# Tap products by two channels side by side in place of four, with a smaller home and a new instruction order

## The chip, the cores and the metric

The kernel runs on one core of one Trainium2 chip. The metric is the device time of one execution in microseconds. The names of the engines are those of the profile: PE is TensorE (its weight loads have a row of their own, PEld), DVE is VectorE, ACT is ScalarE, POOL is GpSimd, SP is SyncE, which here only issues DMAs.

## The reference

One block of a sequence model on 2048 positions of 512 channels in bf16: a state-space convolution and an MLP, each behind a layer norm (the MLP has a second one of its own), each added to its input.

```python
def _A_ref(u, A_re, A_im, B_re, B_im, C_re, C_im, log_dt, Dskip):
    dt = jnp.exp(log_dt)[:, None]
    A = A_re + 1j * A_im;  Bc = B_re + 1j * B_im;  Cc = C_re + 1j * C_im
    logdA = dt * A;  dB = dt * Bc
    l = jnp.arange(L)                                    # L = 2048, rounded to bf16
    P = jnp.exp(logdA[:, :, None] * l[None, None, :])    # 512 x 128 x 2048
    K = jnp.einsum("dn,dnl,dn->dl", Cc, P, dB).real      # the taps, one row per channel
    # y = causal convolution of u with K along the sequence, by FFT of length 4096
    return y + u * Dskip[None, None, :]

def _B_ref(x, w1, b1, w2, b2):                           # 512 -> 1376 -> 512
    y = _layernorm(x, axis=-1)
    h = _gelu(jnp.einsum("bsd,df->bsf", y, w1) + b1)
    return jnp.einsum("bsf,fd->bsd", h, w2) + b2

x = A_u
h = x + _A_ref(_layernorm(x), ...)
h2 = h + _B_ref(_layernorm(h), ...)
```

## The kernel before, in words

All data lives in one SBUF tile `ar` (the "arena"), in which every named buffer is a byte range, and in four PSUM tiles of 128 x 1024 f32 (`ps`), which are handed out as slots. So nearly every row of the profile reads `ar<-ps`, `ps<-ar` or `ar<-ar`, and lines tell the steps apart.

The stages, in the order of their work:

- *Parameters* (L635 to L1070). The raw parameters are loaded and transposed, and `bexps` (L801), `aexps` (L1000 to L1007) and `chain` (L1050 to L1073) make two tables of complex powers: A with 20 rows (a coarse position) and B with 33 rows (a step of 8), each for 128 states (the partitions) and 512 channels in four chunks `c` of 128. Their cosines and sines come from ScalarE (L1068) in `hf` 0 (chunks 0 and 1) and `hf` 1 (chunks 2 and 3), and VectorE multiplies them in (L1030, and L1072 for the A table of chunks 2 and 3). That table lies in `EA2` and `IA2` with the order chunk, group of channels `g` (4), row (20, padded with zeros to 32), channel `i` (32); channel `32 g + i` of the A table belongs to channel `4 i + g` of the columns of the B table.
- *Taps*. K at position `256 h + 8 k + r` is the sum over the states of A times B, which is a matmul for one channel: 20 rows of A as weights, 33 columns of B moving, once for the real and once for the imaginary parts. `kgen` (L1101, L1102) does this for chunks 0 and 1 with four channels in four column groups of the array. `kgen4` (L1132, L1133) does it for chunks 2 and 3 with four channels in one matmul: 4 x 32 = 128 weight columns, 33 x 4 = 132 moving columns, of whose 128 x 132 results only the four blocks on the diagonal (own rows, own channel) are used. All of them are evicted (`evac`, on ScalarE as L542 or on VectorE as L544) into the home `Kg[1]`, and L1142 adds the skip term `Dz`.
- *Spectra of the taps*. `carry` (L1152) shifts rows of the home by four small DMAs, `kspec` (L1167) and `fstage` (L981) transform it, with a trip through DRAM between them (`AK_d`, written and read by `kstage`); `lstage` (L1195, L1214) makes the part for the second half of the sequence. `q` 0 is chunks 0 and 1, `q` 1 is chunks 2 and 3.
- *Convolution*. `unorm` (L947, L949) and `xspec` (L961) norm and transform the input of a half `b` of the sequence, `inverse` multiplies by the taps' spectrum (L1243 to L1251, VectorE) and transforms back (L1259), and a transposing DMA (L1265, `turn`) brings each chunk back to positions.
- *Tail and MLP*. `tail` (L1324 to L1365) finishes the transform, adds the residual and takes the second pair of norms; `mlp` (L1383, L1385 the GELU, L1405, L1407 and the output DMAs) runs for four quarters of 512 positions.

In `stats`, which both norms use, the inverse square root is a power on GpSimd (L926), on which VectorE then waits (L619, L928 in the code).

The order in which each engine gets its instructions is written out. Each step registers an operation with `add`, which numbers it, takes its engine or its two possible engines and a planned cost, and works out its dependencies from the byte ranges. `ORDER` lists the numbers in the order of issue; a negative number `~i` is operation `i` on its second engine. A planner (`Sched.run`) goes through the list with the planned costs; it only decides which PSUM slot a result gets and where TensorE, when it would stand idle in the plan, gets filler matmuls that compute nothing (L1510, at most 24 in a gap). Each engine runs its own list strictly in that order.

Of the kernel before, what the change touches and what calls it, by code (L numbers as in the profile page):

```python
# [15 lines left out]
P = 128  # L16
# [149 lines left out]
class VS(V):  # L166
# [244 lines left out]
def kernel(ctx, tc, A_u, A_A_re, A_A_im, A_B_re, A_B_im, A_C_re, A_C_im, A_log_dt, A_Dskip,  # L411
# [88 lines left out]
    Kg = [take(bf16, NB, 2, 32), at(sc0 - 512, bf16, NB, 4, 2, 32)]  # L500
# [418 lines left out]
    def stats(stv, buf, n, eps1, eps0, pr):  # L919

        sa = lambda k: (lambda: stv.ap()[:, :, k])
        TT(buf[0], stv, stv, ALU.subtract, n=n, aap=sa(1), bap=sa(4), pr=pr)
        STT(buf[2], stv, 512.0 * eps0 / eps1, stv, ALU.add, ALU.add, n=n, aap=sa(2), bap=sa(5), pr=pr)
        STT(buf[1], buf[0], 0.25 * eps1, buf[0], ALU.mult, ALU.mult, n=n, pr=pr)
        STT(buf[1], buf[2], eps1 / 512.0, buf[1], ALU.mult, ALU.add, n=n, pr=pr)
        POOL(0.3, lambda: gp.tensor_tensor(buf[3].ap(), buf[1].ap(), mhalf.ap().to_broadcast([P, n]), ALU.pow), r=[buf[1], mhalf], w=[buf[3]], pr=pr)  # L926
        TT(buf[5], stv, stv, ALU.add, n=n, aap=sa(1), bap=sa(4), pr=pr)
        STT(buf[4], buf[5], -0.5, buf[3], ALU.mult, ALU.mult, n=n, pr=pr)  # L928
# [188 lines left out]
    def kgen4(c, pr):  # L1117
        Ar, Br, Ai, Bi = EA2[c - 2], EB[c], IA2[c - 2], IB[c]
        kg = Kg[1]
        for j0 in range(0, 32, 6):  # L1120
            S.pr = pr + 0.01 * (j0 // 6)
            p = Ps()
            n = min(6, 32 - j0)
            h = (n + 1) // 2
            for b in range(2):
                def fn(e, p=p, j0=j0, b=b, h=h):
                    for jj in range(h):
                        i = j0 + h * b + jj
                        o = pst(p)[:, 512 * b + 132 * jj:512 * b + 132 * jj + 132].rearrange("p (k g) -> p k g", g=4)
                        w = lambda v: v.ap().rearrange("p g a i -> p (g a) i")[:, :, i]  # L1130
                        x = lambda v: v.ap()[:, :, 4 * i:4 * i + 4]
                        pe.matmul(o, lhsT=w(Ar), rhs=x(Br), start=True, stop=False)  # L1132
                        pe.matmul(o, lhsT=w(Ai), rhs=x(Bi), start=False, stop=True)  # L1133
                add("PE", 0.13 * h, fn, r=[EA2, Br, IA2, Bi], w=[p], new=[p] if b == 0 else [], hv=1)
# [4 lines left out]
            def ifn(p=p, h=h):  # L1139
                return pst(p).rearrange("p (b q) -> p b q", b=2)[:, :, 0:132 * h].rearrange("p b (i n) -> p n b i", i=h)  # L1140
            evac(ofn, ifn, 2 * h * 4 * NB, [p], [kg])
        add("DVE", c_dve(128), lambda e: dve.tensor_tensor(kg.ap()[:, 0, :, c & 1, :], kg.ap()[:, 0, :, c & 1, :], Dz.ap()[:, c, :].unsqueeze(1).to_broadcast([P, 4, 32]), ALU.add), r=[kg, Dz], w=[kg])  # L1142

    def kgof(q, g):
        return Kg[0].ap() if q == 0 else Kg[1].ap()[:, :, g]
# [406 lines left out]
```

## Time and profile before

| | us |
|---|---|
| median of 3 runs (lowest, highest) | 235.97 (235.88, 236.08) |
| the profiled execution | 235.89 |
| its span | 234.0 |
| PE busy in it | 200.7 (86%), 2809 matmuls |
| PEld busy | 106.9 (46%) |
| ACT busy | 177.3 (76%), 217 instructions |
| DVE busy | 170.0 (73%), 304 instructions |
| POOL busy | 39.8 (17%) |
| mean granted clock of TensorE | 0.997 |

A line of the groups reads: line, engine, operation, what it writes and reads with shapes, count, busy time in us and mean of one in ns, idle time ahead of it and what ended that. A line of the timeline gives start and length in us. A line of the chain does so too, of the work that ended last. A row of the stretches gives the stretch and its length, then the busy time and the count of each engine, the granted clock, the share of the 16 DMA engines and GB/s.

### The profile page before, as it was taken

The numbers are of one execution on the slowest core, as the hardware profiler recorded it, in microseconds if no ns is written. First come the engines' busy times: TensorE is split into PE (matmuls) and PEld (weight loads), VectorE is DVE, ScalarE is ACT, GpSimd is POOL, SyncE is SP. The second block draws the span as 40 slices with busy tenths as digits, with TensorE's granted clock in tenths as the row PEclk, the third lists the DMA queues.
The fourth block names the chain that finished last, engine by engine and source line by source line (L and its number), as shares of the span: only waits on it lengthen the run. The fifth ranks groups of instructions, "written<-read, shape, count | busy, mean of one in ns | idle before, by whom it ended". The sixth has DMA issues, their size and how long they took to land.

```text
span 234.0 us, 6711 instructions
## 1 busy us (share of the span) xinstructions
PE 200.7 (86%) x2809; PEld 106.9 (46%) x2809; DVE 170.0 (73%) x304; ACT 177.3 (76%) x217; POOL 39.8 (17%) x185
## 2 busy tenths in 40 slices
PE   4206898868888899999989988899999999999993
PEld 2102633325666685456753343344444444444552
DVE  4969989998997764798999889889934884022021
ACT  5999999999999898999989897787275106806600
POOL 7950760000055520040000110100000101000000
PEclk9999999999999999999999999999999999999998
DMA  5692220100000163875589922235632072053103
GB/s 170 165 197 55 59 36 11 37 1 3 3 6 6 30 146 68 244 202 183 112 140 198 311 96 41 49 66 104 114 66 38 0 139 66 0 111 79 34 20 72
DMA packets 39246, 20.33 MB, mean 87 GB/s; under 512 B 26738, under 2 KB 37012, under 8 KB 39216
## 3 DMA queue, kind: packets, MB, share of 16 engines
q1 hardware_dynamic: 38510, 19.28, 36.1%
q0 software_dynamic: 256, 0.30, 0.8%
q8 instruction: 22, 0.36, 0.6%
q10 hardware_dynamic: 450, 0.33, 0.5%
q14 instruction: 8, 0.07, 0.1%
HBM read 8.10 MB, written 4.49 MB: 54 GB/s over the span
## 4 chain that ended last, share of the span: by engine, by line
PE 41%; ACT 13%; DVE 7%; DMA 5%; issue 4%; POOL 3%; SPq 1%; ACTq 0%; DVEq 0%
PE ps L1405 16%; PE ps L1383 13%; ACT ar L542 9%; DMA ar<-ar 3%; PE ps L1329 2%; ACT ar L1068 2%; DMA ar<-AK_d 2%; PE ps L1259 2%; PE ps L981 2%; ACT ar L1385 2%; DVE ar L1248 2%; DVE ar L1243 1%; POOL ar L926 1%; PE ps L961 1%; POOL ar L1466 1%
## 5 line engine op out<-in xcount | busy, mean ns | idle before, releaser
L542 ACT CAST ar<-ps 128x1024 bf16<-128x1024 f32 (+3 forms) x75 | 66.6, 965 | 11.8 <-PE ps L1259 5.1
L1385 ACT ACTIVATE ar<-ps,ar 128x512 bf16<-128x512 f32 (+1 forms) x44 | 28.6, 687 | 25.0 <-PE ps L1383 24.5
L1383 PE MATMUL ps<-ar 128*128 128x512 bf16 (+1 forms) x176 | 40.4, 379 | 1.5 <-ACT ar L542 1.1
L1405 PE MATMUL ps<-ar 128*128 128x512 bf16 (+3 forms) x187 | 39.6, 367 | 0.0
L1068 ACT ACTIVATE ar<-ps 128x1024 bf16<-128x1024 int16 x36 | 34.5, 1058 | 0.5 <-PE ps L1059 0.5
L1407 DVE TENSOR_TENSOR ar<-ps,ar 128x512 bf16<-128x512 f32 (+1 forms) x17 | 10.8, 653 | 29.5 <-PE ps L1405 16.3
L1243 DVE TENSOR_TENSOR ar<-ar 128x2048 bf16<-128x2048 bf16 x24 | 28.8, 1220 | 3.8 <-PE ps L1259 3.0
L1405 PEld LDWEIGHTS <-ar 128*128 128x128 bf16 (+1 forms) x187 | 18.0, 98 | 19.9 <-issue 0.4
L1383 PEld LDWEIGHTS <-ar 128*128 128x128 bf16 (+1 forms) x176 | 17.1, 100 | 21.7 <-issue 3.0
L1059 PE MATMUL ps<-ar 128*32 128x512 f16 (+1 forms) x368 | 21.6, 331 | 5.7 <-ACT ar L1068 5.6
L544 DVE CAST ar<-ps 128x1024 bf16<-128x1024 f32 (+3 forms) x20 | 21.2, 1075 | 7.0 <-PE ps L1133 3.0
L1510 PE MATMUL ps<-ar 128*128 128x512 bf16 x53 | 14.6, 412 | 13.6 <-DMA ar<-in_A_u_dram 12.2
L1030 DVE TENSOR_TENSOR ar<-ar 128x2048 bf16<-128x2048 bf16 x21 | 24.8, 1214 | 0.8 <-ACT ar L1068 0.4
L926 POOL TENSOR_TENSOR ar<-ar 128x4 f32<-128x4 f32 (+1 forms) x6 | 9.3, 1544 | 93.9 <-DVE ar L603 42.2
L801 ACT ACTIVATE ar<-ar 128x1024 bf16<-128x1024 f32 x16 | 15.7, 1041 | 1.1 <-DVE ar L613 1.1
L1059 PEld LDWEIGHTS <-ar 128*32 128x32 f16 x368 | 9.3, 97 | 15.8 <-issue 13.5
L961 PE MATMUL ps<-ar 128*32 128x512 bf16 x256 | 15.9, 380 | 0.2 <-ACT ar L542 0.2
L1259 PE MATMUL ps<-ar 64*128 64x128 bf16 x384 | 13.6, 217 | 1.1 <-ACT ar L542 1.1
L1510 PEld LDWEIGHTS <-ar 128*128 128x128 bf16 x53 | 4.9, 102 | 21.0 <-issue 17.5
L1259 PEld LDWEIGHTS <-ar 64*128 64x128 bf16 x384 | 11.1, 94 | 6.7 <-issue 2.7
L619 DVE SCALAR_TENSOR_TENSOR ar<-ar 128x4 f32<-128x4 f32 (+5 forms) x37 | 10.2, 282 | 5.3 <-POOL ar L926 3.5
L981 PE MATMUL ps<-ar 128*32 128x512 bf16 (+1 forms) x256 | 13.0, 328 | 0.2
(118 smaller groups left out, 293.7 us busy)
## 6 DMA issues: line engine op xcount, KB each, us to landing
ar<-in_A_u_dram SPq DMA_DIRECT2D x4, 512.0 KB
AK_d<-ar SPq DMA_DIRECT2D x4, 512.0 KB
ar<-AK_d SPq DMA_DIRECT2D x4, 512.0 KB
out_dram<-ar SPq DMA_DIRECT2D x30, 64.0 KB
ar<-in_B_w_dram SPq DMA_DIRECT2D x4, 344.0 KB
ar<-ar SPq DMA_DIRECT2D x20, 64.0 KB
ar<-in_B_w_dram SPq DMA_DIRECT2D x2, 640.0 KB
AL_d<-ar POOLq DMA_DIRECT2D x8, 36.0 KB, 4.0
```

What stands on the lines that cost most here:

```text
L542: act.copy(out_fn(), in_fn())
L544: dve.tensor_copy(out_fn(), in_fn())
L961: pe.matmul(pst(p)[32 * cg:32 * cg + 32, 512 * z:512 * z + 512], lhsT=BD.ap()[:, 32 * f + 2 - 2 * jl:32 * f + 34 - 2 * jl], rhs=un[2 * (2 ...
L1030: dve.tensor_tensor(o, o[:, 1].unsqueeze(1).to_broadcast([P] + list(o.shape[1:])), f[:, :, ::-1, ::-1] if rev else f, ALU.mult)
L1059: pe.matmul(pst(p)[32 * g:32 * g + 32, 256 * j:256 * (j + n)].rearrange("p (a b) -> p a b", a=n), lhsT=W2[DELTAS.index(d)].ap(), rhs=S2[g] ...
L1068: add("ACT", c_act(1024), lambda e, o_=o_, i_=i_: act.activation(o_(), i_(), ACT.Sin, scale=SINSC), r=[p, TBL], w=[sc[cs]])
L1243: dve.tensor_tensor(pieces(o).rearrange("p z (a r d) -> p a z r d", a=4, r=2), k, x, ALU.mult)
L1259: pe.matmul(pst(p)[:, 512 * h + 128 * k:512 * h + 128 * k + 128], lhsT=o[z].ap()[rows, k, r, :], rhs=TP[w].ap()[rows, f0 // 2 + k, :], sta ...
L1383: pe.matmul(pst(p)[:fs, 512 * z:512 * z + 512], lhsT=w1s[dc].ap()[:, fc * P:fc * P + fs], rhs=ybuf.ap().rearrange("p (t c) k -> p c t k", ...
L1385: add("ACT", c_act(512, 1), lambda e, p=p, z=z, fc=fc, fs=fs: act.activation(hT.ap()[:fs, fc, :], pst(p)[:fs, 512 * z:512 * z + 512], ACT. ...
L1405: pe.matmul(pst(p)[:, 512 * z + c0:512 * z + c1], lhsT=hT.ap()[:fs, fc, 128 * t:128 * t + 128], rhs=w2s[fc].ap()[:fs, c0:c1], start=(fc == ...
L1510: pe.matmul(slots[z][:, 0:512], lhsT=identb.ap(), rhs=hs[15].ap(), start=True, stop=True)
```

## The change

- `kgen4` is replaced by `kgen2`: each matmul of four channels (128 weight columns by 132 moving columns) becomes two matmuls of two channels (64 by 66), one in the left and one in the right half of the array's columns (`tile_position=(0, 32 * g)`, g = 0 and 2). Real and imaginary parts are accumulated as before. Per chunk these are 128 matmuls in place of 64.
- Half as many results come out, so a PSUM tile holds 12 channels `i` of each group in place of 6: per chunk three evictions (792, 792 and 528 columns) in place of six (five of 792 and one of 264).
- The home `Kg[1]` has 33 x 2 x 2 x 32 entries per partition in place of 33 x 4 x 2 x 32; channel group `g` is read from column `g & 1` (`kgof`). It begins 512 bytes later.
- The planned costs change: kgen2's are 0.14 us per `i` (kgen4's 0.13), and the power in `stats` is planned with 1.5 us in place of 0.3.
- `ORDER` is another list, of 946 in place of 964 operations. Operations 402 to 439 (kgen4) become 402 to 421 (kgen2), and those above 439 have numbers lower by 18. Among the differences: the third DMA that ACT issues, operation 4, stands ahead of the table load (11) in place of behind it; 78 (the eviction of L820, 1024 columns) goes from DVE to ACT and 115 (a copy of 512 columns, L611) from ACT to DVE; the power (162) stands ahead of the memset of L1466 (286) in place of behind it; the read of chunks 0 and 1 from DRAM (374) stands ahead of the carries of chunks 2 and 3 (422 to 425) in place of behind them; the first inverse on PE (521 before, 503 after) stands ahead of the xspec matmuls of the second half in place of behind five of them; the loads of `B_w2` stand ahead of those of `B_w1`.

```diff
-    Kg = [take(bf16, NB, 2, 32), at(sc0 - 512, bf16, NB, 4, 2, 32)]
+    Kg = [take(bf16, NB, 2, 32), at(sc0, bf16, NB, 2, 2, 32)]
...
-        POOL(0.3, lambda: gp.tensor_tensor(buf[3].ap(), buf[1].ap(), mhalf.ap().to_broadcast([P, n]), ALU.pow), r=[buf[1], mhalf], w=[buf[3]], pr=pr)
+        POOL(1.5, lambda: gp.tensor_tensor(buf[3].ap(), buf[1].ap(), mhalf.ap().to_broadcast([P, n]), ALU.pow), r=[buf[1], mhalf], w=[buf[3]], pr=pr)
...
-        for j0 in range(0, 32, 6):
+        for j0 in range(0, 32, 12):
...
-            n = min(6, 32 - j0)
-            h = (n + 1) // 2
+            h = min(12, 32 - j0) // 2
...
-                        o = pst(p)[:, 512 * b + 132 * jj:512 * b + 132 * jj + 132].rearrange("p (k g) -> p k g", g=4)
-                        w = lambda v: v.ap().rearrange("p g a i -> p (g a) i")[:, :, i]
-                        x = lambda v: v.ap()[:, :, 4 * i:4 * i + 4]
-                        pe.matmul(o, lhsT=w(Ar), rhs=x(Br), start=True, stop=False)
-                        pe.matmul(o, lhsT=w(Ai), rhs=x(Bi), start=False, stop=True)
-                add("PE", 0.13 * h, fn, r=[EA2, Br, IA2, Bi], w=[p], new=[p] if b == 0 else [], hv=1)
+                        for g in range(0, 4, 2):
+                            o = pst(p)[32 * g:32 * g + 64, 512 * b + 66 * jj:512 * b + 66 * jj + 66].rearrange("p (k g) -> p k g", g=2)
+                            w = lambda v: v.ap()[:, g:g + 2].rearrange("p g a i -> p (g a) i")[:, :, i]
+                            x = lambda v: v.ap()[:, :, 4 * i + g:4 * i + g + 2]
+                            pe.matmul(o, lhsT=w(Ar), rhs=x(Br), start=True, stop=False, tile_position=(0, 32 * g))
+                            pe.matmul(o, lhsT=w(Ai), rhs=x(Bi), start=False, stop=True, tile_position=(0, 32 * g))
+                add("PE", 0.14 * h, fn, r=[EA2, Br, IA2, Bi], w=[p], new=[p] if b == 0 else [])
...
-            evac(ofn, ifn, 2 * h * 4 * NB, [p], [kg])
+            evac(ofn, ifn, 2 * h * 2 * NB, [p], [kg])
...
-        return Kg[0].ap() if q == 0 else Kg[1].ap()[:, :, g]
+        return Kg[0].ap() if q == 0 else Kg[1].ap()[:, :, g & 1]
```

More of the change, by code (lines that the diff above doesn't have):

```diff
@@ L1115, in kgen, with kgen2 @@
         add("DVE", c_dve(32), lambda e: dve.tensor_tensor(kg.ap()[:, 0, c & 1], kg.ap()[:, 0, c & 1], Dz.ap()[:, c, :], ALU.add), r=[kg, Dz], w=[kg])
-    def kgen4(c, pr):
+    def kgen2(c, pr):
         Ar, Br, Ai, Bi = EA2[c - 2], EB[c], IA2[c - 2], IB[c]
         kg = Kg[1]
-        for j0 in range(0, 32, 6):
-            S.pr = pr + 0.01 * (j0 // 6)
+        for j0 in range(0, 32, 12):
+            S.pr = pr + 0.01 * (j0 // 12)
             p = Ps()
-            n = min(6, 32 - j0)
-            h = (n + 1) // 2
+            h = min(12, 32 - j0) // 2
             for b in range(2):
@@ L1139, in ifn @@
             def ifn(p=p, h=h):
-                return pst(p).rearrange("p (b q) -> p b q", b=2)[:, :, 0:132 * h].rearrange("p b (i n) -> p n b i", i=h)
-            evac(ofn, ifn, 2 * h * 4 * NB, [p], [kg])
-        add("DVE", c_dve(128), lambda e: dve.tensor_tensor(kg.ap()[:, 0, :, c & 1, :], kg.ap()[:, 0, :, c & 1, :], Dz.ap()[:, c, :].unsqueeze(1).to_broadcast([P, 4, 32]), ALU.add), r=[kg, Dz], w=[kg])
+                return pst(p).rearrange("p (b q) -> p b q", b=2)[:, :, 0:66 * h].rearrange("p b (i n) -> p n b i", i=h)
+            evac(ofn, ifn, 2 * h * 2 * NB, [p], [kg])
+        add("DVE", c_dve(64), lambda e: dve.tensor_tensor(kg.ap()[:, 0, :, c & 1, :], kg.ap()[:, 0, :, c & 1, :], Dz.ap()[:, c, :].unsqueeze(1).to_broadcast([P, 2, 32]), ALU.add), r=[kg, Dz], w=[kg])
     def kgof(q, g):
-        return Kg[0].ap() if q == 0 else Kg[1].ap()[:, :, g]
+        return Kg[0].ap() if q == 0 else Kg[1].ap()[:, :, g & 1]
     def carry(q, pr):
@@ L1472 @@
         for c in (2 * q, 2 * q + 1):
-            (kgen if q == 0 else kgen4)(c, 5.1 + 4 * c)
+            (kgen if q == 0 else kgen2)(c, 5.1 + 4 * c)
         carry(q, 9.1 + 8 * q)
```

66 rows, old and new, of the table ORDER are left out of this document.

## The prediction

> **What bounds the kernel now.** I read the page's head first, then the busy time by stretches, then the chain that ended last, then the rows of the stage that the change touches.
>
> ```profile
> span 234.0 us, 6711 instructions
> PE 200.7 (86%) x2809; PEld 106.9 (46%) x2809; DVE 170.0 (73%) x304; ACT 177.3 (76%) x217; POOL 39.8 (17%) x185
> ...
> 77.00:89.70 12.70, 12.70 (x212) 10.23 (x216) 8.12 (x20) 11.64 (x15) 4.23 (x5) 1.00 0.44 105
> 89.70:117.60 27.90, 27.70 (x648) 16.21 (x640) 23.33 (x26) 25.64 (x29) 2.40 (x4) 1.00 0.63 163
> 117.60:154.00 36.40, 32.38 (x397) 15.04 (x390) 32.11 (x50) 32.51 (x41) 2.61 (x3) 1.00 0.54 131
> ...
> 124.00:136.00 12.00, 3.25 (x14) 1.20 (x15) 1.00 0.96 272
> 136.00:154.00 18.00, 2.19 (x10) 0.69 (x8) 1.00 0.17 34
> ```
>
> In the three rows of stretches the columns after the length are PE, PEld, DVE, ACT, POOL. The last two rows are the filler matmuls of L1510 alone (PE, then PEld). From 77.0 to 117.6 TensorE is never free (40.4 of 40.6 us), while VectorE has 4.6 and 4.6 us to spare and ScalarE 1.1 and 2.3. From 117.6 to 154 TensorE lacks 4.0 us, and 24 of its matmuls there are fillers that compute nothing: its slack is before the MLP, not where the taps are made.
>
> ```profile
> 79.05 0.23 PE ps L1132
> ...
> 85.88 3.76 ACT ar L542 x5
> ...
> 93.38 4.98 DMA ar<-AK_d
> ...
> 111.36 6.11 DMA ar<-ar
> ...
> 126.83 0.97 PE ps L1510 x4
> 127.80 0.55 PE ps L1329 x4
> ```
>
> The chain goes from the products of kgen4 (L1132, L1133) through ScalarE's evictions of them, the Dz addition, the four carries, the trip of the spectra through DRAM, the first transpose (L1265) and the evictions held up by it, to the first tail (L1329), ahead of which four fillers ran. Whatever brings that tail and then the MLP forward is worth its time at the end.
>
> **The change part by part.** The sum is made against the profiled execution (235.89 us, span 234.0 us, so 1.89 us around it); the median of the runs is 235.97, 0.08 above.
>
> *Evictions and home.*
>
> ```profile
> L1132 PE MATMUL ps<-ar 128*128 128x132 bf16 x64 | 8.7, 229 | 0.0
> L1133 PE MATMUL ps<-ar 128*128 128x132 bf16 x64 | 8.6, 227 | 0.0
> L1101 PE MATMUL ps<-ar 128*20 128x33 bf16 x256 | 9.8, 247 | 0.0
> L542 ACT CAST ar<-ps 128x792 bf16<-128x792 f32 x7 | 5.5, 871 | 0.2 <-PE ps L1133 0.2
> L544 DVE CAST ar<-ps 128x792 bf16<-128x792 f32 x3 | 2.8, 974 | 1.3 <-PE ps L1133 1.3
> L544 DVE CAST ar<-ps 128x264 bf16<-128x264 f32 x2 | 1.0, 498 | 1.7 <-PE ps L1133 1.7
> L1059 PEld LDWEIGHTS <-ar 128*32 128x32 f16 x368 | 9.3, 97 | 15.8 <-issue 13.5
> L1329 PEld LDWEIGHTS <-ar 128*64 128x64 bf16 x48 | 2.4, 109 | 3.5 <-issue 2.2
> L1383 PEld LDWEIGHTS <-ar 128*96 128x96 bf16 x16 | 1.9, 122 | 1.5
> ```
>
> Twelve evictions (5.5 + 2.8 + 1.0 = 9.3 us) become six: by the new order one of 792 columns on VectorE (0.97), three of 792 (2.6) and two of 528 on ScalarE. The 528s lie between the 264 and 792 rows (0.5 and 0.87); I take 0.6, since 528 is two thirds of 792. Sum 4.8, so 4.5 us less on two engines, 1.7 on ScalarE and 2.8 on VectorE. On the path this is worth little: TensorE has no gap for it to close before 117.6, and VectorE idles there. Bounds: 0, and 2.2 (half of 4.5, were both engines the limit). The halved Dz addition and the smaller home cost nothing: the Dz addition stays one instruction per chunk on an engine with time to spare, and the readers of the home read as many rows as before.
>
> *The products on TensorE.*
>
> ```profile
> 84.00:88.00 4.00, 4.00 (x32) 3.98 (x32) 1.00 0.44 109
> ...
> 70.06 0.29 PE L1101 MATMUL ps<-ar 128*20 128x33 bf16 x4
> ...
> 70.61 0.28 PE L1101 MATMUL ps<-ar 128*20 128x33 bf16 x4
> ```
>
> The first row counts L1132 alone: 32 in 4.00 us, so a pair (four channels) takes 0.125 us and kgen4's 64 pairs 8.0 us. The change makes 256 matmuls of 64 x 66 out of 128 of 128 x 132: per four channels two pairs, one in each half of the array. No row has this shape. The nearest is kgen: its four column groups run side by side (x4 in a row), and from 70.06 to 70.61 (four such rows on) four channels of each group take 0.55 us, so a round of four matmuls takes 0.069 (L1101 and L1102 have one each). 33 columns are a quarter of 132, and yet kgen4's single matmul takes 0.0625: a round costs nearly the same at both sizes. Two rounds per four channels give 0.1375 us, 64 x 0.1375 = 8.8: **+0.8 us**, with no cover, since TensorE is full. Bounds: if each matmul costs only its share of kgen's round (0.069 / 4 = 0.017), 4 x 0.017 x 64 = 4.4 us, -3.6; if the cost follows the weight columns, 0.017 x 64 / 20 = 0.055 each, 14.1 us, +6.1. I stay by the round, since the shapes on either side of the new one both have it.
>
> The Trainium skill, "TensorE: Matmul & The Clock Gate", section "LDWEIGHTS", puts a weight load at columns / 1.2 ns, and "TensorEngine Tiling (Array Packing)", section "Restrictions and Gotchas", says that column tiling excludes Fast Weight Load. By these kgen4's fast load is given up for four slow ones of 53 ns, an estimate of 64 x 4 x 53 ns = 13.7 us if they follow one another. The trace agrees only in part: the loads of 32, 64 and 96 columns last 97, 109 and 122 ns, 0.4 ns per column, half of what that rule says; what they cost one behind the other at this size no row shows. That case is the first rival below.
>
> *The order of the front.*
>
> ```profile
> 1.70 1.28 ACT L536 ACT_TABLE_LOAD   x1 [1.70 <-PEq L1536]
> 1.73 0.41 ACTq L554 DMA_DIRECT2D ar<-in_A_B_re_dram  x1
> ...
> 19.84 0.61 ACT L611 ACTIVATE ar<-ar 128x512 f16<-128x512 f32 x1
> ...
> 7.30 1.22 DVE L544 COPY ar<-ps 128x1024 bf16<-128x1024 bf16 x1
> ...
> 74.47 2.00 ACT L1068 ACTIVATE ar<-ps 128x1024 bf16<-128x1024 int16 x2
> ...
> 73.32 0.17 DVE L619 SCALAR_TENSOR_TENSOR ar<-ar 128x8 f32<-128x8 f32 x1 [1.48 <-POOL ar L926]
> 77.61 1.16 DVE L1072 TENSOR_TENSOR ar<-ar 128x2048 bf16<-128x2048 bf16 x1
> ```
>
> ScalarE carries the path up to its last sine (ends 76.5). In the new order its third DMA issue (0.41) stands ahead of the table load, +0.4; the 1024-column copy of L820 moves from VectorE to it (about +1.0 in its row of casts) and a 512 copy (0.61) leaves: +0.4. So its last sine ends near 77.3. The last product of the taps' inputs (L1072) began only at 77.6, 1.1 us after that sine, since VectorE had lost 1.48 us to GpSimd's power (L926), which was queued behind the memset of L1466; the new order puts it ahead of that memset and eight VectorE instructions before its reader. VectorE then follows ScalarE at once: 77.3 in place of 77.6, **-0.3**. Bounds: -1.1 (ScalarE does not slip) and +0.8 (VectorE, which takes over several GpSimd instructions, is as late as before).
>
> *The order of the middle.*
>
> ```profile
> 89.91 3.35 SPq L1152 DMA_DIRECT2D ar<-ar  x4
> ...
> 89.00:90.00 1.00, 1.00 (x28) 0.50 (x20) 0.34 (x2) 0.90 (x2) 0.00 (x0) 1.00 0.01 2
> ...
> 140.28 1.02 PE L1383 MATMUL ps<-ar 128*128 128x512 bf16 x4 [0.51 <-ACT ar L542]
> ...
> ar<-in_B_w_dram SPq DMA_DIRECT2D x4, 344.0 KB
> ...
> ar<-in_B_w_dram SPq DMA_DIRECT2D x2, 640.0 KB
> ...
> 88.63 2.77 PE L961 MATMUL ps<-ar 128*32 128x512 bf16 x48
> ...
> 118.63 1.07 PE L1259 MATMUL ps<-ar 64*128 64x128 bf16 x32 [0.89 <-ACT ar L542]
> 120.46 1.07 PE L1259 MATMUL ps<-ar 64*128 64x128 bf16 x32 [0.22 <-ACT ar L542]
> ```
>
> On SP's queue the first read of chunks 0 and 1 from DRAM (374) moves ahead of the four carries of chunks 2 and 3 (3.35 us); what it waits for, the write of those chunks, has landed by 89 (the DMA share is 0.01 from 89 to 90), and the carries can't start before 89.9, so nothing behind it waits. Behind the transposes the two 640 KB loads of the MLP's second weights now stand ahead of the four of 344 KB that its first matmul needs: 2.66 MB at the 272 GB/s of the row from 124 to 136 are 9.8 us, from about 122.5 to 132.3, still ahead of an MLP that begins at 140.3 now and near 138.5 then (L1383): 0, with 6 us to spare. On TensorE the first inverse (chunk 0) moves ahead of five eight-matmul blocks of L961 (0.46 each, 2.77 / 6), so its transposes can start some 2 us earlier than 111.36, and the eviction that waited for the 6.11 us transpose is no longer late: the gaps of 0.89 and 0.22 close, **-1.1**. The four fillers ahead of the tail (0.97) go, because their wait was the same row of transposes: **-1.0**. Bounds: 0 for both, and -2.9 more (4.0 us of idle time in the third stretch less the 1.1). After the tail the new order has the same instructions in nearly the same places; I count 0. The new planner cost of the power (1.5 for 0.3) moves only fillers and slots.
>
> Sum: -0.3 + 0.8 - 1.1 - 1.0 = -1.6; 235.9 - 1.6 = **234.3 us**.
>
> **The rivals.**
> 1. *Weight loads set the pace* (the other side). The upper bound of the products, +6.1 in place of +0.8: 234.3 + 5.3 = 239.6. For it: a load of 64 columns is longer than one of 32 (109 against 97 ns), and at this size there is little streaming (66 columns) to hide it. Against: kgen's groups run side by side. It decides from 0.1625 us per four channels (0.1375 + 1.6 / 64); from there on the change is slower. The rule of the Trainium skill's page "TensorE: Matmul & The Clock Gate", section "LDWEIGHTS", speaks for this rival.
> 2. *Nothing closes.* TensorE is full from 77 to 117.6, and the gaps behind have another cause (DMA share 0.96 from 124 to 136). Then -0.3 + 0.8 remains: 236.4, at the edge of no change.
> 3. *Issue sets the pace.* -3.6 in place of +0.8, 4.4 us more; ScalarE has only 3.3 us to spare up to 117.6 and the trip through DRAM keeps its length, so I let half of it through: 232.1.
>
> **How the numbers follow.** Forecast 0.46, rival 3 0.12, rival 2 0.17, rival 1 0.13; 0.12 for the bounds of the front and of the middle that add up to a loss. So faster by over 0.2% (0.47 us, about what a measurement of this kernel can tell) 0.58, within it 0.17, slower 0.25. The forecast alone spans 232.8 to 235.4. The range reaches from rival 3 with a little of the bound of the middle, 231.8, to rival 2 with the front 1.1 later (+0.8 in place of -0.3), 237.5, and 0.3 of slower products, 237.8; rival 1's full price is left out.
>
> **What would show it.** The 256 products of kgen2 should fill 8 to 9.5 us of TensorE, less the blocks of other work among them, against 13 or more in rival 1 and under 5 in rival 3; six evictions of 4.8 us; no wait of VectorE for L926 near 70 us; the last sine near 77.3; the first transpose issued near 109; the first tail near 126 with no fillers ahead; from there to the end as long as before. The prediction is wrong if the products take over 10.5 us, if the gaps ahead of L1259 and the fillers stay, or if the MLP begins as late as now.

## The result and the profile after

The changed kernel takes **251.39 us** (median of 4 runs, 251.21 to 251.71) against 235.94 us (235.88 to 236.08) for the kernel before on the same chip: a ratio of **1.0656**, 95% interval 1.0637 to 1.0674, or 15.45 us more. The prediction said 234.3 us, with 237.8 as its upper end, and named the side wrong. The profiled execution took 251.21 us (span 249.4).

The head of the page after, with the 40 slices of TensorE and of its granted clock (tenths; a slice is 6.2 us):

```profile
span 249.4 us, 6968 instructions
PE 213.6 (86%) x2940; PEld 115.9 (46%) x2940; DVE 175.9 (71%) x308; ACT 172.9 (69%) x209; POOL 35.1 (14%) x183
PE   3225898969888999999999995798999999999993
PEclk9999599999999855799999999799999999999999
```

Before, the clock row was 9 nearly throughout. Now it falls in three places: slice 5 (the front), slices 14 to 17 (the tap products) and slice 26 (the start of the MLP).

Busy time by stretches of the changed kernel (PE, PEld, DVE, ACT, POOL, then the granted clock):

```profile
80.50:84.00 3.50, 3.43 (x60) 3.43 (x62) 1.77 (x6) 1.97 (x2) 2.00 (x2) 1.00 0.20 53
84.00:88.00 4.00, 4.00 (x56) 2.59 (x54) 0.71 (x2) 1.53 (x2) 2.26 (x4) 0.71 0.60 134
88.00:92.00 4.00, 4.00 (x72) 3.98 (x69) 2.44 (x5) 1.01 (x1) 0.00 (x0) 0.50 0.41 116
100.00:104.00 4.00, 4.00 (x50) 1.32 (x52) 2.04 (x5) 1.83 (x3) 0.00 (x0) 0.65 0.14 17
```

TensorE counts as busy all the time, and yet its clock is halved from about 85.7 us, 5 us into kgen2 (80.57 to 99.94), until about 102.8. VectorE and ScalarE stand idle for much of that time.

The groups of the tap products, their loads and their evictions (busy us, mean ns of one); first kgen4's load in the kernel before, then the changed kernel:

```profile
L1132 PEld LDWEIGHTS <-ar 128*128 128x128 bf16 x64 | 8.4, 145 | 0.5 <-issue 0.4
```

```profile
L1132 PE MATMUL ps<-ar 128*64 128x66 bf16 x128 | 15.5, 304 | 0.1
L1132 PEld LDWEIGHTS <-ar 128*64 128x64 bf16 x128 | 14.2, 212 | 3.1 <-issue 2.5 <-DVE ar L1072 0.6
L542 ACT CAST ar<-ps 128x792 bf16<-128x792 f32 x3 | 2.5, 818 | 5.1 <-issue 3.9 <-PE ps L1133 1.2
L542 ACT CAST ar<-ps 128x528 bf16<-128x528 f32 x2 | 1.2, 598 | 6.2 <-PE ps L1133 6.2
L544 DVE CAST ar<-ps 128x792 bf16<-128x792 f32 x1 | 1.0, 983 | 1.7 <-issue 1.7
```

The six evictions take 4.7 us, as forecast. The loads got longer: 212 ns each, where kgen4's load of twice as many columns took 145.

The timeline of PEld, where each row is one load in each column group, at full clock and at half:

```profile
82.05 0.22 PEld L1133 LDWEIGHTS <-ar 128*64 128x64 bf16 x2
...
82.60 0.22 PEld L1132 LDWEIGHTS <-ar 128*64 128x64 bf16 x2
...
90.57 0.22 PEld L1133 LDWEIGHTS <-ar 128*64 128x64 bf16 x2
...
91.12 0.22 PEld L1132 LDWEIGHTS <-ar 128*64 128x64 bf16 x2
```

The first two rows shown are five rounds apart, and so are the last two: 0.55 us, so 0.110 us for a round of two products at either clock. Four channels are two rounds, 0.22 us. Over whole runs of products (first to last start) it is 0.227 to 0.249 us, and the 64 groups of four channels take 14.9 us. kgen4's took 8.5 (0.133 us).

The chain of work that ended last: first one block of the kernel before, then the changed kernel from the front to the MLP:

```profile
76.92 1.04 PE ps L1167 x16
```

```profile
25.63 5.91 PE ps L1000 x102
...
79.33 1.20 DVE ar L1072
80.57 0.33 PE ps L1132 x2
...
86.27 1.83 PE ps L1167 x15
...
100.06 1.83 PE ps L961 x16
...
138.18 0.62 PE ps L1329 x4
...
156.63 1.02 ACT ar L542
157.69 5.13 PE ps L1383 x16
```

A block of L1167 takes 1.83 us where it took 1.04 before, and 16 matmuls of L961 take 1.83 us where 48 took 2.77: other work that runs at half clock. The first tail is 10.4 us later than before. Behind it another 5 us are lost, at the start of the MLP.

The places compared, in us, from the records of each line in the profiled executions (L1132's first start to its last end; the first start of L1329; the ends of L1072 and of TensorE):

| run | last L1072 ends | tap products | first tail | TensorE ends |
|---|---|---|---|---|
| before | 78.8 | 79.0 to 88.6 | 127.7 | 230.0 |
| changed | 80.5 | 80.6 to 99.9 | 138.2 | 245.5 |
| shape_old_order | 78.8 | 79.0 to 96.2 | 136.2 | 242.7 |
| order_alone | 79.8 | 79.9 to 92.3 | 129.4 | 236.9 |
| eviction_earlier | 80.3 | 80.4 to 99.9 | 137.9 | 240.1 |
| old_front_new_rest | 78.9 | 79.1 to 91.6 | 130.2 | 232.4 |
| old_front_kgen2 | 78.8 | 79.0 to 98.2 | 136.5 | 239.1 |
| old_front_kgen2_unit_stride | 78.7 | 79.0 to 91.2 | 128.7 | 230.8 |
| adjacent_layout | 79.1 | 79.3 to 91.4 | 127.8 | 229.9 |

### The profile page after: what moved, and what is told of

It reads as the page before. It is cut to its first block, busy times and chain, and to the rows that moved or that the text cites. A ratio compares the mean times of both kernels' runs of the same rounds, so it can differ in the third digit from the quotient of the medians.

```text
span 249.4 us, 6968 instructions
## 1 busy us (share of the span) xinstructions
PE 213.6 (86%) x2940; PEld 115.9 (46%) x2940; DVE 175.9 (71%) x308; ACT 172.9 (69%) x209; POOL 35.1 (14%) x183
## 4 chain that ended last, share of the span: by engine, by line
PE 62%; DVE 16%; ACT 12%; issue 4%; DMA 3%; POOL 1%; SPq 1%; ACTq 0%; POOLq 0%
PE ps L1383 15%; PE ps L1405 13%; ACT ar L1068 6%; PE ps L961 5%; PE ps L981 4%; PE ps L1259 4%; PE ps L1132 3%; DMA ar<-ar 3%; DVE ar L1243 3%; PE ps L1133 3%; PE ps L1059 3%; PE ps L1510 3%; PE ps L1000 2%; ACT ar L542 2%; PE ps L1329 2%
## 5 line engine op out<-in xcount | busy, mean ns | idle before, releaser
L542 ACT CAST ar<-ps 128x1024 bf16<-128x1024 f32 (+4 forms) x69 | 62.5, 954 | 27.4 <-PE ps L1133 7.4
L1383 PE MATMUL ps<-ar 128*128 128x512 bf16 (+1 forms) x176 | 41.4, 389 | 4.7 <-ACT ar L542 4.5
L1405 PE MATMUL ps<-ar 128*128 128x512 bf16 (+3 forms) x187 | 40.1, 367 | 0.9 <-ACT ar L542 0.8
L544 DVE CAST ar<-ps 128x1024 bf16<-128x1024 f32 (+3 forms) x20 | 22.3, 1128 | 11.2 <-PE ps L961 4.2
L1383 PEld LDWEIGHTS <-ar 128*128 128x128 bf16 (+1 forms) x176 | 17.8, 102 | 26.3 <-issue 7.8
L1405 PEld LDWEIGHTS <-ar 128*128 128x128 bf16 (+1 forms) x187 | 17.9, 98 | 20.7 <-issue 1.8
L1510 PE MATMUL ps<-ar 128*128 128x512 bf16 x56 | 15.6, 415 | 9.3 <-DMA ar<-in_A_u_dram 8.6
L926 POOL TENSOR_TENSOR ar<-ar 128x4 f32<-128x4 f32 (+1 forms) x6 | 7.5, 1255 | 97.1 <-DVE ar L603 42.0
L961 PE MATMUL ps<-ar 128*32 128x512 bf16 x256 | 18.6, 411 | 0.4 <-ACT ar L542 0.4
L801 ACT ACTIVATE ar<-ar 128x1024 bf16<-128x1024 f32 x16 | 15.6, 1043 | 0.8 <-DVE ar L613 0.8
L1132 PEld LDWEIGHTS <-ar 128*64 128x64 bf16 x128 | 14.2, 212 | 3.1 <-issue 2.5
L1132 PE MATMUL ps<-ar 128*64 128x66 bf16 x128 | 15.5, 304 | 0.1
L1133 PE MATMUL ps<-ar 128*64 128x66 bf16 x128 | 15.3, 302 | 0.0
L1133 PEld LDWEIGHTS <-ar 128*64 128x64 bf16 x128 | 14.3, 213 | 0.0
L1259 PE MATMUL ps<-ar 64*128 64x128 bf16 x384 | 13.5, 217 | 0.6 <-DVE ar L544 0.4
```

Of the source, the lines that this page charges most:

```text
L542: act.copy(out_fn(), in_fn())
L961: pe.matmul(pst(p)[32 * cg:32 * cg + 32, 512 * z:512 * z + 512], lhsT=BD.ap()[:, 32 * f + 2 - 2 * jl:32 * f + 34 - 2 * jl], rhs=un[2 * (2 ...
L1132: pe.matmul(o, lhsT=w(Ar), rhs=x(Br), start=True, stop=False, tile_position=(0, 32 * g))
L1133: pe.matmul(o, lhsT=w(Ai), rhs=x(Bi), start=False, stop=True, tile_position=(0, 32 * g))
L1259: pe.matmul(pst(p)[:, 512 * h + 128 * k:512 * h + 128 * k + 128], lhsT=o[z].ap()[rows, k, r, :], rhs=TP[w].ap()[rows, f0 // 2 + k, :], sta ...
L1383: pe.matmul(pst(p)[:fs, 512 * z:512 * z + 512], lhsT=w1s[dc].ap()[:, fc * P:fc * P + fs], rhs=ybuf.ap().rearrange("p (t c) k -> p c t k", ...
```

## The experiments

All ratios are to the kernel before, run beside each on the same chip (its medians there 235.99 to 236.71 us).

**1. The shape alone and the order alone.**

```
shape_old_order: ORDER of before
- 402, 403, 405, -405, 406, 408, 409, 407, ... 439      (38 entries of kgen4)
+ 402, 403, 405, 404, 406, -408, 408, 412, ... 421      (20 entries of kgen2)
order_alone: ORDER of after
- 402, 403, 405, 406, -405, ... 421                     (20 entries of kgen2)
+ 402, 403, 404, 405, 406, ... 439                      (38 entries of kgen4)
```

> kgen2 in the order of before: in place of kgen4's 38 entries stand kgen2's 20 at the matching places, all else in the old order. Theory A (the shape is the loss: 64-column weight loads come one behind the other, 0.055 us each, and the array is then so little used that its clock is halved): the products take 14 us and more in place of 8.0, the clock falls to 0.5 some 3.4 us after they begin, the first tail comes 8 to 10 us later than at 127.8, and the time is 244 to 247 us. Theory B (the new order is the loss, the shape costs at most the 0.8 us of the prediction): 235 to 238 us, clock 1.00 throughout.

> kgen4 in the new order: kgen2's 20 entries are opened into kgen4's 38 (two products' halves for each, the added evictions on the other of the two engines), all else as in the new order. Theory A: the products take 8 us at clock 1.00; what is left of the loss is the front, whose last sine ended 2.8 us later and whose last L1072 ended 1.8 us later than before, and perhaps part of the 5 us between the first tail and the MLP: 237 to 241 us. Theory B: 249 to 252 us.

Measured: shape_old_order 248.40 us (1.051, 1.0478 to 1.0542), order_alone 243.14 us (1.0293, 1.0254 to 1.0332). Both parts lose. In shape_old_order the products took 15.1 us and the clock fell, as theory A says, and the first tail came 8.5 us late; but the end came 12.7 us late, more than the theory says. There are now 69 fillers of L1510 in place of 53, and further waits behind the tail; why was not followed up. order_alone lies above the 237 to 241 us of theory A: the order by itself costs 7.0 us, of which 1.0 at the last L1072, 0.6 more up to the first tail, and 5 behind it. Both together cost 15.4, less than the sum of 19.2.

What TensorE waited for between 80 and 165 us in order_alone (total, times, longest):

```profile
PE ps L1383 <- ACT ar L542: 4.5, 2, 4.0
PE ps L1132 <- DVE ar L544: 0.8, 1, 0.8
PE ps L1405 <- ACT ar L542: 0.8, 1, 0.8
```

The waits ahead of L1259 that the prediction meant to close are gone, and one of 4.0 us in front of L1383 has come. The second row is new too: kgen4's products wait 0.8 us until VectorE has evicted a PSUM tile of theirs. In this list they take 10.0 us (0.157 us for four channels) in place of 8.5.

**2. What sets the clock, and what sets the pace.**

```
double_stream
- o = ...[32*g:32*g+64, 512*b+66*jj:512*b+66*jj+66]
+ o = ...[32*g:32*g+64, 512*b+66*jj:512*b+66*jj+132]     (two times 66)
- x = ...[:, :, 4*i+g:4*i+g+2]
+ x = ...[:, :, 4*i+g:4*i+g+2].unsqueeze(1).to_broadcast([P, 2, NB, 2])
groups_in_turn
- for jj in range(h): ... for g in range(0, 4, 2): (products)
+ for g in range(0, 4, 2): for jj in range(h): (products)
```

> The changed kernel, but each kgen2 matmul streams its 66 columns twice (132; the second 66 fall on the next channel's place and are overwritten by it). Weights, their loads and the count of instructions stay. Theory A with the clock set by how much is streamed: the pace stays 0.22 us for four channels, since the loads set it, the clock stays 1.00 from 80 to 100, and the blocks of L961 and L1167 among the products run at full speed: 3 to 5 us less than the changed kernel, 246 to 248 us. If the clock falls for another reason (column groups, the strided loads): clock 0.5 as before and 251 to 252 us. If streaming set the pace: 0.4 us for four channels and over 258 us.

> The changed kernel, but in each block of channels all products of the first column group are issued ahead of those of the second, so that two groups can hardly run side by side. If the weight loads share one way in (0.055 us each, whatever the group): the products still take 0.22 us for four channels and the time stays within 1 us of 251.4. If each column group has its own pace (0.11 us for a product) and side by side is what halves it: 0.44 us for four channels, the products take 28 us and the time is 262 to 268 us.

Measured: double_stream 253.61 us (1.0721, 1.067 to 1.0771), groups_in_turn 256.15 us (1.0838, 1.0798 to 1.0879). In double_stream the clock stays up, with the same loads and the same column groups:

```profile
84.00:88.00 4.00, 4.00 (x58) 3.67 (x58) 1.06 (x2) 0.13 (x1) 1.75 (x3) 1.00 0.46 99
88.00:92.00 4.00, 4.00 (x60) 3.46 (x54) 2.38 (x5) 2.31 (x3) 0.00 (x0) 1.00 0.19 54
```

So neither the loads nor the column groups by themselves make the clock fall; with twice as much streamed it stays up. The time was expected to fall by 3 to 5 us and rose by 2.2, because the pace is not the loads' alone: four channels took 0.31 us. That is about 4.8 us more for the 64 groups. The full clock gave part of it back: the blocks of L1167, L961 and L981 ahead of the first L1259 take 16.0 us in place of 19.0. groups_in_turn lies between its two cases, 0.30 to 0.37 us for four channels on the whole; the timeline of its loads shows why:

```profile
81.00 0.20 PEld L1132 LDWEIGHTS <-ar 128*64 128x64 bf16 x1
81.11 0.20 PEld L1133 LDWEIGHTS <-ar 128*64 128x64 bf16 x1
...
81.78 0.23 PEld L1133 LDWEIGHTS <-ar 128*64 128x64 bf16 x2
81.89 0.24 PEld L1132 LDWEIGHTS <-ar 128*64 128x64 bf16 x2
```

Where one group runs alone (x1), a product comes every 0.11 us; where the two groups overlap at the seams of blocks (x2), each of them still does so. Each column group has its own pace of 0.11 us here. A single way in that all loads share, at 0.055 us each, does not fit: one group alone would then come every 0.055 us.

**3. The new order's own loss.**

```
eviction_earlier (one entry, six places)
- 704, 720, 656, 710, 714, 640, 715, 455, 660
+ 704, 455, 720, 656, 710, 714, 640, 715, 660
old_front_new_rest
  ORDER = (before, up to its first 402) + (order_alone with that eviction moved, without those entries)
```

> The changed kernel with one entry of the order moved six places forward: ScalarE's eviction of the lstage of features 0 to 3 of chunks 2 and 3 (entry 455) stands ahead of VectorE's second inverse (720, 714, 715) in place of behind it; no engine's own sequence changes. In the new order this eviction waited 3.7 us for that VectorE work, TensorE stood idle 4.0 us behind it and then ran 3 us at half clock. If that one dependency is the loss between first tail and MLP: the 4-us gap shrinks below 1 us, no half clock near 158 to 161 us, 3.5 to 5 us less than the changed kernel, 246 to 248 us. If another wait takes its place (the slot is not what TensorE lacks): 250 to 252 us.

> kgen4, the order of before up to its first kgen4 entry, then the new order with the eviction moved as in eviction_earlier. If the new middle is worth what the prediction said (-2.1 us): 233.5 to 234.5 us. If it is worth nothing, since TensorE has the same work and no idle time to give back: 235.5 to 237 us, the first tail near 127.7 to 128.5.

Measured: eviction_earlier 245.41 us (1.0368, 1.0319 to 1.0417), 6.0 us less than the changed kernel (6.8 by the ratios) and a little more gain than expected; old_front_new_rest 237.89 us (1.0051, 1.0025 to 1.0077). The changed kernel's timeline, first ScalarE's row, then TensorE's (start, us, and in brackets the idle time ahead and what ended it):

```profile
156.63 1.01 ACT L542 CAST ar<-ps 128x1024 bf16<-128x1024 f32 x1 [3.68 <-DVE ar L619]
```

```profile
153.04 0.62 PE L1259 MATMUL ps<-ar 64*128 64x128 bf16 x16
157.69 0.59 PE L1383 MATMUL ps<-ar 128*128 128x512 bf16 x1 [4.03 <-ACT ar L542]
```

and the same stretch by windows, first of the changed kernel, then of eviction_earlier:

```profile
152.00:156.00 4.00, 1.66 (x21) 0.83 (x20) 3.97 (x7) 0.95 (x2) 0.00 (x0) 1.00 0.00 0
156.00:160.00 4.00, 2.31 (x6) 0.86 (x6) 2.47 (x5) 2.58 (x4) 0.00 (x0) 0.67 0.00 0
```

```profile
152.00:156.00 4.00, 3.75 (x31) 1.81 (x30) 3.97 (x6) 4.00 (x6) 0.00 (x0) 1.00 0.00 0
156.00:160.00 4.00, 4.00 (x39) 1.92 (x38) 3.85 (x8) 3.08 (x5) 0.00 (x0) 1.00 0.69 129
```

One eviction on ScalarE stood in the list behind VectorE's second inverse and waited for it; TensorE, out of PSUM slots, stood for 4.0 us; and its clock was half from 157.4 to 160.8 us, most of it behind the gap. With the eviction moved ahead, gap and half clock are gone. The second run lies above both of its cases, with the first tail 2.5 us later than before. Of these, 1.6 us are kgen4's products, which take 10.1 us in this list too, with the same wait of 0.8 us for an eviction. So this run does not show what the new middle is worth with kgen2.

**4. Columns or stride.**

```
full_weights
- o = ...[32*g:32*g+64, ...66 columns]; w = v[:, g:g+2] "(g a) i"[:, :, i]; tile_position=(0, 32*g)
+ o = ...[all 128, ...66 columns];      w = v            "(g a) i"[:, :, i]; (no tile_position)
unit_stride_weights
- w = ...rearrange("p g a i -> p (g a) i")[:, :, i]
+ w = ...rearrange("p g a i -> p (g a i)")[:, 64*i:64*i+64]
```

> The changed kernel with 128 weight columns in each of the 256 products in place of 64, without column groups; two of four channels are thereby left out of the result. If a load costs by its columns (0.86 ns each, as the 64-column ones seem to): 0.11 us a product, 28 us, 262 us or more. If loads of the full width come as fast as kgen4's (at most 0.062 us each): 12 to 16 us for the products and, with twice as much of the array in use, clock 1.00: 245 to 251 us. If streaming sets the pace of such products: 8 to 10 us and 242 to 245 us.

> The changed kernel with each product's 64 weight columns taken from adjacent elements in place of every 32nd one; the taps of chunks 2 and 3 are thereby left out of the result. If the stride makes the loads slow: 0.14 to 0.18 us for four channels in place of 0.22 and 244 to 249 us. If the column group itself sets the pace: 0.22 us, clock 0.5 again, and within 1.5 us of 251.4.

Measured (one run each): full_weights 248.62 us, as its second case said, and unit_stride_weights 242.86 us, below its first. The load and matmul groups with adjacent columns:

```profile
L1132 PE MATMUL ps<-ar 128*64 128x66 bf16 x128 | 10.1, 262 | 0.0
L1132 PEld LDWEIGHTS <-ar 128*64 128x64 bf16 x128 | 9.2, 136 | 1.7 <-issue 1.3 <-ACT ar L542 0.4
```

The load falls from 212 to 136 ns, four channels from 0.233 to 0.149 us, and the clock stays at 1.00 through the products: 8.5 us gained by the place of the weights alone. Here the products cost little more than the 0.1375 us of the prediction. Full-width strided loads took 0.063 to 0.070 us a product with 66 columns streamed, which is kgen4's pace with 132, so at the full width too the strided load sets the pace. The Trainium skill, "SBUF — State Buffer", section "Door 1: The DMA port swizzle", says that SBUF has lines of 16 bytes and that each access that goes over to a new line pays for it; a bf16 column every 64 bytes pays at each column. The traces agree in kind: strided and adjacent loads take 212 and 136 ns at 64 columns, and 145 and 96 ns at 128 (kgen4, and kgen4_unit_stride below). No run tried a stride in between, so the 16 bytes themselves are not shown here.

**5. The parts put together.**

```
kgen4_unit_stride (before)
- w = ...rearrange("p g a i -> p (g a) i")[:, :, i]
+ w = ...rearrange("p g a i -> p (g a i)")[:, 128*i:128*i+128]
old_front_kgen2: kgen2, ORDER = (before, up to its first 402) + (eviction_earlier, without those entries)
old_front_kgen2_unit_stride: old_front_kgen2 with the edit of unit_stride_weights
adjacent_layout: old_front_kgen2 with
- EA2, IA2 = at(EA2lo, bf16, 2, 4, 32, 32), ...      (chunk, group, row a, index i)
+ EA2, IA2 = at(EA2lo, bf16, 32, 8, 32), ...         (index i, chunk and group, row a)
- w = ...rearrange("p g a i -> p (g a) i")[:, :, i]
+ w = v.ap()[:, i, 4*c-8+g:4*c-6+g].rearrange("p g a -> p (g a)")
...
```

> The kernel before with kgen4's 128 weight columns taken from adjacent elements in place of every 32nd one; the taps of chunks 2 and 3 are thereby left out of the result. Products of 128 columns take 0.063 to 0.066 us whether 132 or 66 columns are streamed, so the strided load may set the pace of kgen4 too. If so, the products fall to about 0.058 us each, 128 of them save 0.8 to 1.0 us, and the time is 235.0 to 235.5 us. If streaming sets it: 0.066 us as before and no difference.

> The changed kernel (kgen2) with the order of before up to the first tap product, then the new order with the eviction moved as in eviction_earlier. If the new front's loss of 1.0 to 1.6 us at the start of the products goes through to the end: 243.8 to 244.4 us (eviction_earlier 245.4), and 6 us above old_front_new_rest (237.9), which differs from it by kgen4 alone. If something later takes it up: 245 to 246 us.

> old_front_kgen2 with the 64 weight columns of each product taken from adjacent elements; the taps of chunks 2 and 3 are thereby left out of the result. If strided loads (and the half clock that follows from the slow products) are the whole price of the shape: 0.147 us for four channels, clock 1.00 through the products, 236 to 238.5 us, no more than 1 us from old_front_new_rest with kgen4. If the shape costs by itself, through its column groups or its evictions: 240 us or more.

> old_front_kgen2 with the two inputs of the taps of chunks 2 and 3 stored so that each product's 64 weight columns lie side by side (index, channel group, frequency row in place of channel group, row, index); ScalarE's exponentials and sines and VectorE's products of those inputs write four adjacent elements at a time in place of 32 or 128, and everything is computed. If that writing costs nothing: 0.147 us for four channels at clock 1.00 and 235.2 to 236.2 us, as old_front_kgen2_unit_stride (235.7). If ScalarE or VectorE pay for it: each of the ten exponentials and sines or the five products (1.2 us each) that gets longer stands on the path ahead of the taps, so 0.1 us more each is about 1 us, and a product twice as long puts the time above 240 us.

Measured: kgen4_unit_stride 235.77 us (0.9981, 0.9954 to 1.0008); old_front_kgen2 244.54 (1.0328, 1.0275 to 1.0382); old_front_kgen2_unit_stride 235.65 (0.996, 0.9936 to 0.9985); adjacent_layout 235.81 (0.9977, 0.9951 to 1.0003). The second and the last came as expected; the first lies just above its better case, the third just below its own.

kgen4's products did get faster with adjacent columns, 0.116 to 0.123 us for four channels in place of 0.132 to 0.134, but the kernel's time cannot be told from before. In one order, kgen2 costs 6.65 us more than kgen4 (244.54 against 237.89) with strided weights, and 2.2 us less (235.65) with adjacent ones: the two-channel form is no loss, the stride is. (In that order kgen4 pays 1.6 us for the waits of its products, and kgen4 with adjacent weights was not run in it.) adjacent_layout computes everything and stores its inputs so that the columns lie side by side. Together with the old front and the moved eviction it undoes the 15.4 us; L1072 pays 0.05 us a product for the new layout (1258 ns, 1204 before):

```profile
L1072 DVE TENSOR_TENSOR ar<-ar 128x2048 bf16<-128x2048 bf16 x5 | 6.2, 1258 | 0.0
```

Against the kernel before its interval just reaches 1, so a gain over it is not shown.

## Why the prediction was wrong, by its own steps

- **The products** (+0.8 us) are the first step that failed. Their number of columns and of rounds was weighed, their stride was not. I took kgen's round to hold for the shape; it nearly holds with adjacent weights (0.149 us for four channels) and not with strided ones (0.233). The mis-sized term measures +6.4 us (14.9 - 8.5), close to the upper bound of 6.1 that I kept for rival 1 with a chance of 0.13 and left out of the range. Rival 1 had the mechanism, loads that set the pace, but its bound came out by luck. Its price of 0.86 ns a weight column comes from kgen, whose loads are strided too (20 columns, each 256 bytes from the next), and kgen2's round of 2 x 64 columns in 0.110 us gives 0.86 again; but adjacent columns cost 0.58 ns (0.0745 us a round) and full-width strided ones 0.5, so the number of columns alone is not the cause. The reading "0.125 us, 8.0 us" for kgen4 was also low: a stretch's count takes in the matmuls that reach over its ends; start to start it is 0.133 us, 8.5 us.
- **The clock** had no term at all, though the profile has a row for it. It fell with the strided products and stayed up with the adjacent ones. In the pair old_front_kgen2 and old_front_kgen2_unit_stride the first matmul of L1259 starts 8.8 us apart; the pace accounts for 5.4 of it (14.9 against 9.5). Most of the rest are other blocks at half clock: between the first product and that matmul, the same 304 matmuls of L1167, L961 and L981 take 19.3 us in the one and 16.0 in the other, start to start. No run had the strided products at full clock and nothing else changed, so this share is read within one pair and not isolated. The Trainium skill, "TensorE: Matmul & The Clock Gate", section "What's actually happening", describes a gate that throttles after an idle window of about 3.4 us. The 4.0-us gap at the start of the MLP, and the half clock of 3.4 us that sets in at 157.4, near its end, agree with that; the tap products do not fit an idle window, since TensorE was 4.00 of 4.00 us busy while the clock fell.
- **The front** (-0.3) came out at +1.7 in the changed kernel and +1.0 in order_alone. The part on VectorE was right: L1072 starts 0.03 us after the last sine, not 1.1. But the last sine ends at 79.3, not 77.3, since two things ahead of it were not followed. On SP's queue the load of C_im had gone from third to fourth place, and L815, which waits for it, starts 2.1 us later. The copy of L820 was costed by its own length and not by who waits for it: on ScalarE it starts 1.5 us after L815's end, behind exponentials (L801), where on VectorE it started after 0.6. The changed kernel's timeline, TensorE, then ScalarE and VectorE:

```profile
7.39 1.46 PE L815 MATMUL ps<-ar 128*128 128x128 bf16 x12 [1.31 <-DMA ar<-in_A_C_im_dram]
...
25.63 0.62 PE L1000 MATMUL ps<-ar 128*32 128x256 f16 x8 [0.68 <-DMA ar<-ar]
```

```profile
10.32 0.99 ACT L542 COPY ar<-ps 128x1024 bf16<-128x1024 bf16 x1
```

```profile
11.35 1.89 DVE L603 TENSOR_TENSOR ar<-ps,ar 128x512 f32<-128x512 bf16 x3 [0.87 <-ACT ar L542]
```

  L815 started at 5.26 before, that chain of VectorE at 8.55 and L1000 at 22.66. The half clock from 24.3 to 31.1 us adds nothing to it: from the first L1000 to the last sine are 53.6 us, before 53.8. The old front gives back 0.9 us (245.41 to 244.54).
- **The middle** (-1.1 and -1.0) did not show up in order_alone. The gaps ahead of L1259 did close, but from the first product to the first tail are 49.5 us in place of 48.8. The matmuls between the two are nearly the same ones (8 more of L961, 8 fewer of L981, 5 fillers for 4); what grew by 1.5 us are kgen4's own products, in a list written for half as many evictions. So kgen4 in the new order is no clean test of this step. With kgen2 and adjacent weights the same stretch takes 48.6 us (adjacent_layout) and 49.7 (old_front_kgen2_unit_stride), though the products are 1.0 us longer than kgen4's were before: an estimate of 1.2 and 0.1 us gained, from two profiled executions, out of the 2.1 forecast. The fillers ahead of the tail did not go altogether: two stand there in the changed kernel, four before.
- **After the tail** (0) cost 5 us in order_alone and in the changed kernel. "The same instructions in nearly the same places" was not looked at place by place; a single place was worth 6 us.
- Evictions (4.7 us, nothing on the path), SP's read and the loads of the MLP came as said.

Put together, by the differences of the ratios (times 235.94, since the runs lie on several chips): 15.45 us are 6.8 of that eviction (1.0656 to 1.0368), 0.9 of the front (to 1.0328, within the runs' uncertainty), 6.5 of strided products with the clock that they take along (to 1.0051), and 1.2 that the rest of the new order costs with kgen4. By the medians the same steps are 6.0, 0.9, 6.65 and 1.95. In the last two steps kgen4's products take 10.1 us and not 8.5; against an unhindered kgen4 the shape's price would be nearer 8 us and that of the rest of the order nearer nothing (an estimate; no run has it). The code plans kgen2 with 0.14 us for four channels; with products that do take 0.149, the new order with the old front and the moved eviction ends at 235.65.

## What to carry to other kernels

- When a matmul is cut into smaller ones, look at the stride of the stationary operand as well as its number of columns: loads whose columns lie 64 bytes apart set the pace of the products of chunks 2 and 3 here, at 64 columns and at 128, and a layout with adjacent columns took 8.7 us off (244.54 to 235.81 us; 8.3 by the ratios).
- A busy TensorE is not a used one. Work out how much is streamed per us when an edit makes products smaller, and read the clock row of the stage: other work in it pays too.
- In an order that is written anew, an instruction that "hardly moves" has still to be followed across engines: whose result does it wait for now, and who has no buffer until it is done.

## What the runs showed of the hardware

- The granted clock halved with TensorE at 4.00 of 4.00 us busy. In units of full-width columns streamed per ns (66 x 64/128 x 2 in a round, for kgen2), worked out from the paces above, it fell at 0.57 (0.117 us a round) and at 0.41 (groups_in_turn, about 0.159 us for two products), and it stayed at 1.00 at 0.86 (double_stream), 0.89 (unit_stride_weights) and 1.02 (full_weights). That is not yet a rule with an edge: by the same count kgen streams only 0.30 (33 x 20/128 x 4 in a round of 0.069 us), and in the kernel before the clock stood at 1.00 while it ran from 68.9 to 71.3 us, a shorter stretch. What exactly lets the clock fall stays open. adjacent_layout was at half clock from 79.45 to 82.86 us in its profiled run; that began 0.2 us after its first product, so what led to it lies, in the main, ahead of the products.
- Strided 64-column products keep 0.110 us a round at half clock as at full clock (rows of PEld at 82 and at 91 us).
- Two column groups with strided loads run side by side without slowing each other: 0.11 us per product in each, alone or together (groups_in_turn).
- Full-width strided loads carry twice the columns in less time (0.063 us) than 64-column ones in a column group (0.110 us).
